# Second feed-forward of an attention kernel: one tile at a time, or two tiles side by side

## The chip, the cores and the metric

The kernel runs on one core of a Trainium2 chip. The metric is the device time of one execution in microseconds (us). The engines are TensorE (PE; its weight loads are PEld), VectorE (DVE), ScalarE (ACT), GpSimd (POOL) and SyncE (SP), whose queue issues all DMA of this kernel.

## The reference

Attention within chunks of 64 tokens, then two feed-forwards on 4608 tokens of width 512. The change is in the second one, which takes `x`, the first one's output:

```
def _moe2_ref(x, w1, w2, w3, w_out):      # x: 4608 x 512
    a = x @ w1                            # 512 x 1024
    b = x @ w2                            # 512 x 1024
    h = a * b @ w3                        # 1024 x 1024
    return (h @ w_out).astype(np.float32) # 1024 x 512
```

Both kernels fold `w3 @ w_out` into one matrix of 1024 x 512 beforehand, so this stage is `(a * b) @ wf`.

## The kernel before

Every fp32 number is split into a high and a low part, and each product of matrices runs as three matmuls into one accumulation: high by high, high by low, low by high (`mm3`, lines 105 to 107). `split` (lines 100 and 101) makes the parts, the high one on ACT, the low one on DVE.

The 4608 tokens are 9 tiles of 512. The second feed-forward goes through the tiles in the order `PASS2` = 8, 2, 3, 4, 5, 6, 7, 0, 1, and in each tile through 8 units `f`, each of them 128 columns of `w1` and of `w2`: 72 units `u`. In a unit, the two products `a` and `b` are computed together by the scheme of Strassen and Winograd on 2 x 2 blocks: seven block products instead of eight. The blocks of the token operand are the two halves of the width by the two halves of the tile, so a block has 256 tokens, and sums of blocks are formed once per tile: `B11`, `B21`, `T2`, `T1`, `T3`, `B22`, `T4`, the seven operands `X`. The four weight operands of a unit are blocks of `w1`, `w2` and sums of them. They are prepared in an earlier stage, stored in DRAM (`sd`), and loaded once by `pump()`, line 316: three tiles `w` of 512 KB and one tile `s4` of 256 KB per unit. For all 8 units that is 24 of the 25 `w` slots, and there they stay for all tiles.

`ab_mm(u)` issues the seven products of a unit: 7 x 2 x 3 = 42 matmuls that move 256 columns. They go into four PSUM banks of two pools (`ps_hh`, `ps_aa`), which ACT (`x1`, line 474) and DVE (`d`, `e`, lines 482 to 501) empty while they combine the products. Line 662 multiplies `a` by `b`. `ab_split(u)` splits the result into one of the two halves of the ring `phl`. `out_mm(u - 1)` then issues the output product of the unit before: 4 accumulators `acc` x 3 = 12 matmuls that move 512 columns of `wf`. At the last unit of a tile each accumulator is copied into an `o` tile (even ones by ACT, odd ones by DVE; three buffers) and stored.

So PE's order in the steady state is 42 narrow matmuls of unit u, 12 wide ones of unit u - 1, and so on. At a tile's last unit `x_op` is called behind each product and overwrites the operand just used with that of the next tile; the sums for it were made by POOL (`x_sums`).

Order on each engine is program order: the stage is under a manual schedule, and each engine's queue is served in the order in which the code issues. In the first unit the last output product of the first feed-forward (`x2_mm`, 24 wide matmuls) lies between.

Of the kernel before, what the change touches and what calls it, by code (L numbers as in the profile page):

```python
# [17 lines left out]
P = 128  # L18
NT = 4608
TT = 512  # L20
# [25 lines left out]
ORDER3E = "S1sT25a3cACoobBoxodoDyoo"  # L46
ORDER3X = "12sq5a3clhAbCrmdBDxy"
FOLD = 1
N3 = 13


# [4 lines left out]
def chunk_attention_two_ffn(  # L56
# [246 lines left out]
    def pump():  # L303

        n = 0
        while lq and lq[0] in staged:
            key = lq[0]
            if key[1] == 3 and isinstance(key[0], tuple):
                if not free(s4s, 1):
                    break  # L310
                t = new_s4(key)
            elif free(slots, 1):
                t = new_w(key)
            else:
                break
            nc.sync.dma_start(out=f32(t), in_=staged.pop(lq.pop(0)))
            n += 1
        return n


    qks, vs, att = {}, {}, {}
# [294 lines left out]
    def fold(b, part):  # L616

        if part == 0:
            wf_ps[b] = bank_a()
        a = W["w3", 2 * b + part // 2]  # L620
        for j in range(2 * part, 2 * part + 2):
            o = W["wo2", j]
            m = slice(P * (j % 4), P * (j % 4) + P)
            mm3(wf_ps[b], (a[:, 0, m], a[:, 1, m]), (o[:, 0], o[:, 1]), j == 0, j == 7)
        if part % 2:
            load_w3()
        if part == 3:
            hi, lo = (one.tile([P, TT], F32R, tag=tag, name="wfo") for tag in ("s5", "s6"))
            p = wf_ps.pop(b)
            nc.scalar.activation(hi, p, AF.Copy)  # L630
            nc.vector.tensor_tensor(out=lo, in0=p, in1=f32(hi), op=ALU.subtract)
            nc.sync.dma_start(out=wfd[b][:, 0], in_=f32(hi))
            nc.sync.dma_start(out=wfd[b][:, 1], in_=f32(lo))
            if b == FB2 - 1:
                done_with(("wo2", j) for j in range(FB2))
                done_with(["x2o"])


    order = PASS2
    phv, phl = {}, {}  # L640

    def load_wf(f):
        if f in (2, 3):
# [7 lines left out]
            parts = d[:, 0], d[:, 1]  # L651
        W["wf", f] = parts

    def ab_mm(u):
        f = u % FB2
        last = f == FB2 - 1 and u + 1 < NTILE * FB2
        z = Seven(("w12", f), (bank_h, bank_h, bank_a, bank_a), True, x_op if last else None)
# [5 lines left out]
        phv[u] = z.e  # L663

    def ab_split(u):
        if u == 0:
            phl["both"] = one.tile([P, 8, 256], F32R, tag="g", name="phl")
        t = phl["both"][:, 4 * (u % 2):4 * (u % 2) + 4].rearrange("p (s t) k -> p s (t k)", s=2)
        split(t, phv.pop(u), nc.vector)
        phl[u] = t  # L670

    def out_mm(u):
        n, f = order[u // FB2], u % FB2
# [3 lines left out]
        w, p = W["wf", f], phl.pop(u)  # L677
        for b in range(4):
            m = slice(P * b, P * b + P)
            mm3(acc[b], (p[:, 0, m], p[:, 1, m]), w, f == 0, f == FB2 - 1)  # L680
            if f == FB2 - 1:
                t = wk.tile([P, TT], F32, tag="cw", name="o", bufs=3)
                if b % 2 == 0:
                    nc.scalar.activation(t, acc[b], AF.Copy)
                else:
                    nc.vector.tensor_copy(t, acc[b])
                r0 = n * TT + b * P
                nc.sync.dma_start(out=out[r0:r0 + P, :], in_=t)


    with tc.manual_schedule():
# [34 lines left out]
        for i in range(NG):  # L726
            if i == GA:
                sq.extend(("wo2", j) for j in range(FB2))
                for g in range(GA, G1):
                    sq.extend((nm, 2 * g + e) for nm in ("in", "out") for e in range(2))  # L730
                    lq.extend((("in", g), p_) for p_ in range(4))
                    lq.extend(("out", 2 * g + e) for e in range(2))
                lq.extend(("wo2", j) for j in range(FB2))
                sq.extend(("w3", j) for j in range(N3))
                for f in range(FB2):
                    sq.extend((nm, f) for nm in ("w1", "w2"))
                    if N3 + f < 16:
                        sq.append(("w3", N3 + f))
                    lq.extend((("w12", f), p_) for p_ in range(4))
                st_load()  # L740
            if i == iB + FOLD - 1:
                load_w3()
# [78 lines left out]
            if ps == 1:  # L821
                if nth == 0 and nxt in xs:
                    if not pre:
                        xr = one.tile([P, CC, TT], F32R, tag="xf", name="xr")
                        pre.update((op, xr[:, 2 * j:2 * j + 2]) for j, op in enumerate(("B11", "B21")))
                    for op in pre:
                        nc.sync.dma_start(out=f32(pre[op]), in_=xs[nxt][op])
                if nth == 0 and nxt not in xs:
                    if pre:
                        pre.clear()  # L830
                        xf = one.tile([P, CC, TT], F32, tag="xf", name="xf")
                    nc.sync.dma_start(out=xf, in_=x2d[order[0]] if nxt is None else xd[nxt])
# [6 lines left out]
        U2 = NTILE * FB2  # L839
        for f in (4, 5, 6):  # L840
            load_wf(f)
        for u in range(U2 + 1):
            if u < FB2:
                need(*((("w12", u), p_) for p_ in range(4)))
            pump()
            if u == FB2 - 1:
                load_wf(FB2 - 1)
            if u < U2:
                ab_mm(u)
                if u == 0:  # L850
                    x2_mm(NG - 1, 0)
                    x2_mm(NG - 1, 1)
                ab_split(u)
            if u >= 1:
                out_mm(u - 1)
            if u == 0:
                load_wf(2)
                load_wf(3)
            f = u % FB2
            if u < U2 - FB2:  # L860
                if f == 1:
                    nc.sync.dma_start(out=xf, in_=x2d[order[u // FB2 + 1]])
                if f == 4:
                    x_sums()


# [47 lines left out]
```

## Time and profile before

| | |
|---|---|
| timed runs | 1526.86, 1527.42, 1532.41 us; median 1527.42 |
| span of the profiled execution, first to last instruction | 1524.5 us |
| time of the profiled execution by the clock of the timed runs | not recorded; the span lies 2.9 us below the median |
| PE busy | 1470.5 us, 96% of the span |
| DVE, ACT, POOL busy | 1099.5, 773.8 and 261.8 us |
| DMA | 248.82 MB, 163 GB/s over the span |

The profile records one execution. A busy matmul in it is counted from its start to its modelled end, and the next one starts before that end, so how fast PE works is read from the distances between starts, and whether it works without a pause from its list of waits.

### The profile page before, as it was taken

What the parts mean: (1) busy time and instruction counts of PE and PEld (TensorE: products, weight loads), DVE (VectorE), ACT (ScalarE), POOL (GpSimd) and SP (SyncE); (2) the same over time, 40 slices, a digit from 0 to 9 for tenths busy, and PEclk for the clock granted to TensorE, in tenths of its full rate; (3) what the DMA queues carried; (4) which work ended last, traced back from release to release, by engine and by line L of the source; (5) the groups of instructions that cost most, each with busy time, mean ns of one, the idle gap of its engine ahead of it and who ended that gap; (6) DMA issues with size and microseconds to landing.
All of it is one profiled execution on the core that took longest, in us unless ns stands there. A gap on an engine that the chain in (4) does not pass through costs nothing.

```text
span 1524.5 us, 28710 instructions
## 1 busy us (share of the span) xinstructions
PE 1470.5 (96%) x11340; PEld 1318.9 (87%) x11340; DVE 1099.5 (72%) x1876; ACT 773.8 (51%) x1349; POOL 261.8 (17%) x206
## 2 busy tenths in 40 slices
PE   4789999999999999999999999999999999999998
PEld 3778788888888889888888888999999999999998
DVE  6986798888888887777777777665655646656564
ACT  4877788787887876555555556221221212212121
POOL 0222222222222222222221122101101011010000
PEclk7999999999999999999999999999999999999999
DMA  7654655565664718998888775601101101011000
GB/s 241 204 198 141 213 174 204 163 243 193 213 212 138 242 63 310 359 328 320 299 315 299 274 279 191 258 9 48 56 1 56 37 20 57 1 56 56 1 29 28
DMA packets 103814, 248.82 MB, mean 163 GB/s; under 512 B 11520, under 2 KB 23552, under 8 KB 102016
## 3 DMA queue, kind: packets, MB, share of 16 engines
q1 hardware_dynamic: 103680, 246.99, 46.9%
q8 instruction: 90, 1.47, 0.4%
q14 instruction: 44, 0.36, 0.1%
HBM read 151.78 MB, written 95.16 MB: 162 GB/s over the span
## 4 chain that ended last, share of the span: by engine, by line
PE 68%; DVE 12%; ACT 12%; DMA 5%; issue 2%; POOL 1%; SPq 0%; DVEq 0%; ACTq 0%; POOLq 0%
PE acc L106 9%; PE acc L105 9%; PE acc L107 9%; PE ps_hh L105 9%; PE ps_hh L107 8%; PE ps_hh L106 8%; PE ps_aa L105 5%; PE ps_aa L106 5%; PE ps_aa L107 5%; ACT t L551 2%; ACT L368 2%; ACT t L550 1%; ACT L551 1%; POOL ex L377 1%; DVE ex L362 1%
## 5 line engine op out<-in xcount | busy, mean ns | idle before, releaser
L564 POOL TENSOR_TENSOR g<-t,g 128x512 fp32r<-128x512 f32 x144 | 196.5, 1385 | 584.4 <-ACT g L563 464.4
L100 ACT ACTIVATE phl<-e 128x512 fp32r<-128x512 f32 x72 | 45.5, 632 | 364.8 <-DVE e L662 356.7
L105 PE MATMUL acc<-g,w 128*128 128x512 f32 x576 | 228.1, 396 | 0.0
L106 PE MATMUL acc<-g,w 128*128 128x512 f32 x576 | 226.8, 394 | 0.1
L107 PE MATMUL acc<-g,w 128*128 128x512 f32 x576 | 224.8, 390 | 0.0
L107 PE MATMUL ps_hh<-T,w 128*128 128x256 f32 x680 | 193.3, 284 | 4.7 <-DVE w L198 4.7
L105 PE MATMUL ps_hh<-T,w 128*128 128x256 f32 x680 | 196.8, 289 | 0.9 <-ACT x L474 0.9
L106 PE MATMUL ps_hh<-T,w 128*128 128x256 f32 x680 | 193.1, 284 | 0.0
L105 PE MATMUL ps_hh<-B,w 128*128 128x256 f32 x620 | 180.2, 291 | 5.1 <-DVE t L555 3.3
L482 DVE TENSOR_TENSOR d<-x,ps_hh 128x512 f32<-128x512 f32 x134 | 91.8, 685 | 120.6 <-PE ps_hh L107 103.7
L106 PE MATMUL ps_hh<-B,w 128*128 128x256 f32 x620 | 176.7, 285 | 0.0
L107 PE MATMUL ps_hh<-B,w 128*128 128x256 f32 x620 | 176.6, 285 | 0.0
L107 PEld LDWEIGHTS ps_hh<-T,w 128*128 128x128 f32 x680 | 131.0, 193 | 5.3 <-DVE w L198 5.1
L105 PEld LDWEIGHTS ps_hh<-T,w 128*128 128x128 f32 x680 | 131.0, 193 | 4.5 <-ACT x L474 1.5
L106 PEld LDWEIGHTS ps_hh<-T,w 128*128 128x128 f32 x680 | 131.1, 193 | 0.7
L105 PEld LDWEIGHTS ps_hh<-B,w 128*128 128x128 f32 x620 | 119.7, 193 | 12.4 <-DVE t L555 3.8
L107 PEld LDWEIGHTS acc<-g,w 128*128 128x128 f32 x576 | 108.3, 188 | 22.9
L106 PEld LDWEIGHTS acc<-g,w 128*128 128x128 f32 x576 | 108.6, 189 | 22.2 <-POOL g L564 3.1
L105 PEld LDWEIGHTS acc<-g,w 128*128 128x128 f32 x576 | 108.6, 188 | 19.5
L106 PEld LDWEIGHTS ps_hh<-B,w 128*128 128x128 f32 x620 | 119.9, 193 | 3.9
L106 PE MATMUL ps_aa<-T,w 128*128 128x256 f32 x432 | 122.5, 284 | 0.4 <-DVE T L101 0.4
L107 PE MATMUL ps_aa<-T,w 128*128 128x256 f32 x432 | 122.4, 283 | 0.0
(139 smaller groups left out, 3598.4 us busy)
## 6 DMA issues: line engine op xcount, KB each, us to landing
w<-sd SPq DMA_DIRECT2D x63, 512.0 KB, 7.3
sd<-raw SPq DMA_DIRECT2D x104, 256.0 KB, 4.4
qk<-in_q_dram SPq DMA_DIRECT2D x36, 256.0 KB, 4.2
qk<-in_k_dram SPq DMA_DIRECT2D x36, 256.0 KB, 4.6
vt<-in_v_dram SPq DMA_DIRECT2D x72, 128.0 KB, 3.0
x2a<-x2o SPq DMA_DIRECT2D x36, 256.0 KB, 2.6
x2a<-x2a SPq DMA_DIRECT2D x36, 256.0 KB, 5.5
x2d<-x2a SPq DMA_DIRECT2D x36, 256.0 KB, 3.1
```

Source lines behind the costliest of these rows:

```text
L100: nc.scalar.activation(dst[:, 0], src, AF.Copy)
L105: nc.tensor.matmul(ps, a[0], b[0], start=first, stop=False)
L106: nc.tensor.matmul(ps, a[0], b[1], start=False, stop=False)
L107: nc.tensor.matmul(ps, a[1], b[0], start=False, stop=last)
L362: nc.vector.tensor_tensor(out=ex[:, :, c], in0=ps[c], op=ALU.subtract, in1=mx[:, :, c].unsqueeze(2).to_broadcast([P, HP, 64]))
L368: nc.scalar.activation(ex, ex, AF.Exp, scale=SCALE)
L377: (nc.vector if early else nc.gpsimd).tensor_tensor(out=ex, in0=ex, in1=rc.unsqueeze(2).to_broadcast([P, 2 * HP, 64]), op=ALU.mult)
L482: nc.vector.tensor_tensor(out=two(self.d), in0=self.x1.unsqueeze(1).to_broadcast([P, 2, 256]), in1=two(p26), op=ALU.add)
L550: nc.scalar.activation(t, t, AF.Abs)
L551: nc.scalar.activation(t, t, AF.Sin, scale=-TWO_PI, bias=half_pi)
L564: nc.gpsimd.tensor_tensor(out=lo, in0=r, in1=f32(hi), op=ALU.subtract)
```

## The change

Tile 8 is still done alone, by `alone_mm`, as before. The other eight tiles are taken in pairs: (2, 3), (4, 5), (6, 7), (0, 1). The blocks of the token operand are now the two halves of the width by the two tiles of the pair, so that a block has 512 tokens, and each of the seven products moves 512 columns and fills one PSUM bank. Each operand has two tiles of 512 columns, one per 128 rows of the half width (`X2`): the old `X[op]`, and one more `w` slot.

For each unit of a pair `duo_mm` issues 42 matmuls of 512 columns. The first tile's result is split into the ring at once and goes to `out_mm`, 12 matmuls, behind the products of the following unit. The second tile's result is kept in `pst` (four `w` slots). After the 8 units, the eight output products of the second tile follow one upon the other, each behind a `late_split` of the kept result, and in the same steps the operands of the next pair are split (`duo_op`).

The slots that hold `X2`, `pst` and the sources of a pair (`duo_load`) leave ten for weights. So the weights of all 8 units are no longer resident: `pump()` loads those of a unit again for every pair, at most `AHEAD` = 2 units ahead of the unit in work, and `release(u)` frees a unit's slots when its products are issued.

```diff
     def pump():
         n = 0
-        while lq and lq[0] in staged:
+        while lq:
             key = lq[0]
+            kept = (("w12", key[0][1] % FB2), key[1]) if key[0][0] == "w12" else key
+            if kept not in staged or (kept != key or key[0][0] == "w12") and key[0][1] > unit[0] + AHEAD:
+                break
...
-            nc.sync.dma_start(out=f32(t), in_=staged.pop(lq.pop(0)))
+            nc.sync.dma_start(out=f32(t), in_=staged[kept])
+            lq.pop(0)
             n += 1
...
+    def duo_load(duo):
+        a, b = duo
...
+        nc.sync.dma_start(out=y["A"], in_=x2d[a])
+        nc.sync.dma_start(out=y["lo"], in_=x2d[b][:, 0:2])
+        nc.sync.dma_start(out=y["hi"], in_=x2d[b][:, 2:4])
+
+    def duo_sums():
+        b11, b21, b12, b22, t1, t2 = y["A"][:, 0:2], y["A"][:, 2:4], y["lo"], y["hi"], spare, y["t2"]
+        nc.gpsimd.tensor_tensor(out=t1, in0=b12, in1=b11, op=ALU.subtract)
+        nc.gpsimd.tensor_tensor(out=t2, in0=b22, in1=t1, op=ALU.subtract)
+        nc.gpsimd.tensor_tensor(out=b12, in0=b22, in1=b12, op=ALU.subtract)
+        y["v"] = dict(B11=b11, T1=t1, T3=b12, B21=b21, T2=t2, B22=b22, T4=b21)
+
+    def duo_op(op, c):
+        v = y["v"]
+        split(X2[op][c], v[op][:, c], nc.vector)
+        if op == "T2":
+            nc.vector.tensor_tensor(out=v["T4"][:, c], in0=v["B21"][:, c], in1=v["T2"][:, c], op=ALU.subtract)
+
+    def duo_mm(u, j):
+        f = u % FB2
+        w = [W[("w12", u), i] for i in range(4)]
+        def prod(a, i, op):
+            ps = (bank_h, bank_a)[n_bank[0] // 2 % 2]()
+            n_bank[0] += 1
+            for c in range(2):
+                m = slice(256 * i + P * c, 256 * i + P * c + P)
+                mm3(ps, (w[a][:, 0, m], w[a][:, 1, m]), (X2[op][c][:, 0], X2[op][c][:, 1]), c == 0, c == 1)
+            return ps
...
+        nc.scalar.activation(x1, prod(0, 0, "B11"), AF.Copy)
+        add(d0, x1, prod(0, 1, "B21"))
+        add(d1, x1, prod(2, 0, "T2"))
+        p7 = prod(2, 1, "T3")
+        add(e0, d1, p7)
+        add(e0, e0, prod(1, 1, "T4"))
+        nc.vector.tensor_tensor(out=e0, in0=d0, in1=e0, op=ALU.mult)
+        t = ring(j)
+        nc.scalar.activation(t[:, 0], e0, AF.Copy)
+        add(e1, d1, prod(1, 0, "T1"))
+        add(d1, e1, p7)
+        nc.vector.tensor_tensor(out=t[:, 1], in0=e0, in1=f32(t[:, 0]), op=ALU.subtract)
+        add(e1, e1, prod(3, 0, "B22"))
+        nc.vector.tensor_tensor(out=pst[f // 2][:, f % 2], in0=d1, in1=e1, op=ALU.mult)
+
+    def late_split(j, f):
+        split(ring(j), pst[f // 2][:, f % 2], nc.vector)
...
-        for u in range(U2 + 1):
-            if u < FB2:
-                need(*((("w12", u), p_) for p_ in range(4)))
...
+        for u in range(FB2):
+            take_weights(u)
...
+            e = alone_mm(u, after)
...
+            if u:
+                out_mm(u - 1, *jobs[u - 1])
...
+            release(u)
+            if u == 1:
+                duo_load(DUOS[0])
...
+            if u == 3:
+                duo_sums()
+            if u in (4, 5, 6):
+                for op in (OPS[0:3], OPS[3:5], OPS[5:7])[u - 4]:
+                    duo_op(op, 1)
+        j = FB2
+        for s, duo in enumerate(DUOS):
+            for f in range(FB2):
+                u = FB2 * (s + 1) + f
+                take_weights(u)
+                duo_mm(u, j)
...
+                out_mm(j - 1, *jobs[j - 1])
+                release(u)
+                if s + 1 < len(DUOS):
+                    if f == 1:
+                        duo_load(DUOS[s + 1])
+                    if f == 4:
+                        duo_sums()
+                j += 1
+            late_split(j, 0)
+            for f in range(FB2):
+                out_mm(j - 1, *jobs[j - 1])
+                if f + 1 < FB2:
+                    late_split(j + 1, f + 1)
+                for op, c in halves[2 * f:2 * f + 2]:
+                    duo_op(op, c)
+                j += 1
+        out_mm(j - 1, *jobs[j - 1])
```

How this moves instructions, engine by engine. First PE, in the kernel before, in a unit of the second feed-forward: the end of the seventh product (`T4`) and the first two accumulators of the output.

```order
L105 MATMUL ps_aa<-T_172,w 128x256
L106 MATMUL ps_aa<-T_172,w 128x256
L107 MATMUL ps_aa<-T_172,w 128x256
L105 MATMUL acc_16175<-wf,phl 128x512
L106 MATMUL acc_16175<-wf,phl 128x512
L107 MATMUL acc_16175<-wf,phl 128x512
L105 MATMUL acc_16176<-wf,phl 128x512
L106 MATMUL acc_16176<-wf,phl 128x512
```

The same place in the changed kernel, in a unit of a pair: the seventh product is now `B22`, with the weight tile `s4` (printed `s`), and its second operand tile stands in a `w` slot.

```order
L106 MATMUL ps_aa_15247<-B22_171,s4_15032 128x512
L107 MATMUL ps_aa_15247<-B22_171,s4_15032 128x512
L108 MATMUL ps_aa_15247<-B22_171,s4_15032 128x512
L106 MATMUL ps_aa_15247<-w_11481,s4_15032 128x512
L107 MATMUL ps_aa_15247<-w_11481,s4_15032 128x512
L108 MATMUL ps_aa_15247<-w_11481,s4_15032 128x512
L106 MATMUL acc0_14752<-wf_11280,phl_11369 128x512
L107 MATMUL acc0_14752<-wf_11280,phl_11369 128x512
L108 MATMUL acc0_14752<-wf_11280,phl_11369 128x512
```

The narrow matmuls are gone from there: one wide matmul stands for the two narrow ones of two tiles, and PE has 8738 rows instead of 10082.

Next DVE, in the kernel before, around the end of a tile: the unit's combination, the split (line 101), and the two output copies (line 686) between units.

```order
L501 TENSOR_TENSOR e<-e,ps_aa 128x512
L662 TENSOR_TENSOR e<-d,e 128x512
L101 TENSOR_TENSOR phl<-e,phl 128x512
L686 COPY o<-acc_15589 128x512
L686 COPY o<-acc_15591 128x512
L482 TENSOR_TENSOR d<-x_16125,ps_hh 128x512
L492 TENSOR_TENSOR e<-d,ps_aa 128x512
```

DVE in the changed kernel, at the end of a pair's units, where the second tile's outputs begin: line 750 keeps the last result, line 102 is the split of a kept result (`phl<-w`) or of half an operand of the next pair, line 688 the two output copies of the first tile, line 718 the `T4` subtraction.

```order
L750 TENSOR_TENSOR w<-d_14346,e_14348 128x512
L102 TENSOR_TENSOR phl<-w,phl 128x512
L688 COPY o<-acc_13885 128x512
L688 COPY o<-acc_13887 128x512
L102 TENSOR_TENSOR phl<-w,phl 128x512
L102 TENSOR_TENSOR B_166<-xa_11469,B_166 128x512
L102 TENSOR_TENSOR w<-xa_11469,w 128x512
L102 TENSOR_TENSOR phl<-w,phl 128x512
L102 TENSOR_TENSOR B_167<-xa_11469,B_167 128x512
L102 TENSOR_TENSOR w<-xa_11469,w 128x512
L102 TENSOR_TENSOR phl<-w,phl 128x512
L102 TENSOR_TENSOR T_168<-w,T_168 128x512
```

The copies now stand between the splits of two neighbouring output steps, and operand halves stand between the splits of the later ones.

Last SP's queue, in the kernel before, at the start of the stage: the last weights that are ever loaded (`w`, `s4`), the next tile's source, the last block of `wf`, and the first tile's four stores.

```order
L646 DMA wf_11412<-wfd3_157 128x512
L646 DMA wf_11413<-wfd3_157 128x512
L316 DMA w_11416<-sd28_10389 128x1024
L316 DMA s4_11418<-sd29_10393 128x512
L862 DMA xf_10344<-x2d2_142 128x2048
L650 DMA w_11842<-wfd7_161 128x1024
L688 DMA out_0_dram<-o_11988 128x512
L688 DMA out_0_dram<-o_11994 128x512
```

SP's queue in the changed kernel, at the end of a pair: the weights of a unit ahead, four stores of the first tile, four of the second, and the next unit's weights.

```order
L320 DMA w_12686<-sd42_8746 128x1024
L320 DMA w_12688<-sd42_8928 128x1024
L320 DMA w_12690<-sd43_8932 128x1024
L320 DMA s4_12692<-sd44_8936 128x512
L690 DMA out_0_dram<-o_12699 128x512
L690 DMA out_0_dram<-o_12705 128x512
L690 DMA out_0_dram<-o_12711 128x512
L690 DMA out_0_dram<-o_12717 128x512
L690 DMA out_0_dram<-o_12921 128x512
```

Where the queue held only tile sources and stores after the first tile, weight loads now stand between them to the last pair.

## Rows read from the trace of the kernel before

**Rows 1.** Page: span, PE, and granted clock by slice.

```profile
span 1524.5 us, 28710 instructions
...
PE 1470.5 (96%) x11340; PEld 1318.9 (87%) x11340; DVE 1099.5 (72%) x1876; ACT 773.8 (51%) x1349; POOL 261.8 (17%) x206
...
PEclk7999999999999999999999999999999999999999
```

**Rows 2.** PE's waits, 930 to 1524 us: who, for whom, total, times, longest.

```profile
PE ps_aa L106 <- DVE T L101: 0.4, 1, 0.4
```

**Rows 3.** Timeline of PE, one unit: start, duration, instruction.

```profile
1307.17 0.28 PE L105 MATMUL ps_hh<-B,w 128*128 128x256 f32 x1
...
1312.20 0.40 PE L105 MATMUL acc<-wf,phl 128*128 128x512 f32 x1
...
1313.59 0.39 PE L105 MATMUL acc<-wf,phl 128*128 128x512 f32 x1
...
1314.95 0.28 PE L105 MATMUL ps_hh<-B,w 128*128 128x256 f32 x1
```

**Rows 4.** Timeline of PE, 24 output matmuls of the first unit, ninth and successor.

```profile
961.23 0.39 PE L107 MATMUL acc<-g,w 128*128 128x512 f32 x1
...
964.85 0.28 PE L105 MATMUL ps_hh<-B,w 128*128 128x256 f32 x1
```

**Rows 5.** Windows: busy time by engine, granted clock, DMA share, GB/s.

```profile
960.00:965.00 5.00, 5.00 (x25) 4.13 (x24) 3.52 (x6) 0.00 (x0) 0.00 (x0) 1.00 1.02 409
965.00:970.00 5.00, 5.00 (x44) 5.00 (x43) 3.23 (x6) 1.01 (x2) 0.00 (x0) 1.00 1.03 370
...
1300.00:1350.00 50.00, 50.00 (x354) 47.06 (x353) 29.96 (x48) 11.55 (x22) 3.09 (x3) 1.00 0.12 43
```

**Rows 6.** Groups by line, second feed-forward; last, POOL's one sum at 983 us.

```profile
L101 DVE TENSOR_TENSOR phl<-e,phl 128x512 fp32r<-128x512 f32 x63 | 44.0, 698 | 44.0 <-ACT phl L100 44.0
...
L100 ACT ACTIVATE phl<-e 128x512 fp32r<-128x512 f32 x63 | 39.8, 632 | 317.0 <-DVE e L662 317.0
...
L438 POOL TENSOR_TENSOR xf<-xf x1: 1298/1298/1298, 983.3 to 983.3; 128x512 f32<-128x512 f32 x1
```

**Rows 7.** Timeline of DVE: two independent operations, then two dependent ones.

```profile
1078.66 0.69 DVE L101 TENSOR_TENSOR T<-spare,T 128x512 fp32r<-128x512 f32 x1
1079.26 0.69 DVE L101 TENSOR_TENSOR T<-xf,T 128x512 fp32r<-128x512 f32 x1
...
1094.57 0.69 DVE L501 TENSOR_TENSOR e<-e,ps_aa 128x512 f32<-128x512 f32 x1 [0.29 <-PE ps_aa L107]
1095.29 0.69 DVE L662 TENSOR_TENSOR e<-d,e 128x512 f32<-128x512 f32 x1
```

**Rows 8.** Timeline of the kernel's end: accumulator copies and stores.

```profile
1517.23 0.39 PE L105 MATMUL acc<-w,phl 128*128 128x512 f32 x1
...
1518.13 0.60 ACT L684 ACTIVATE o<-acc 128x512 f32<-128x512 f32 x1 [1.36 <-PE acc L107]
...
1518.75 3.21 SPq L688 DMA_DIRECT2D out_dram<-o  x4
...
1519.74 0.39 PE L107 MATMUL acc<-w,phl 128*128 128x512 f32 x1
1520.91 0.69 DVE L686 COPY o<-acc 128x512 f32<-128x512 f32 x1 [1.41 <-DMA out_dram<-o]
```

**Rows 9.** Line 688 (output stores), 1000 to 1524 us.

```profile
DMA to landing us min/median/max: 2.0/2.1/4.3
```

**Rows 10.** Line 316 (weight loads), 930 to 980 us.

```profile
DMA to landing us min/median/max: 3.7/7.4/10.1
```

**Rows 11.** Timeline of SP's queue near the first unit's end.

```profile
966.18 1.10 SPq L646 DMA_DIRECT2D wf<-wfd  x2
...
970.66 0.80 SPq L646 DMA_DIRECT2D wf<-wfd  x2
971.51 0.42 SPq L316 DMA_DIRECT2D w<-sd  x1
```

More of the change, by code (lines that the diff above doesn't have):

```diff
@@ L48 @@
 FOLD = 1
+AHEAD = 2
 N3 = 13
@@ L315, in pump @@
                 break
-            nc.sync.dma_start(out=f32(t), in_=staged.pop(lq.pop(0)))
+            nc.sync.dma_start(out=f32(t), in_=staged[kept])
+            lq.pop(0)
             n += 1
         return n
+    unit = [0]
     qks, vs, att = {}, {}, {}
@@ L635, in fold @@
                 done_with(("wo2", j) for j in range(FB2))
-                done_with(["x2o"])
-    order = PASS2
-    phv, phl = {}, {}
+    ALONE, DUOS = PASS2[0], [(2, 3), (4, 5), (6, 7), (0, 1)]
+    UNITS = FB2 * (1 + len(DUOS))
+    phl = {}
     def load_wf(f):
@@ L652, in load_wf, with ring, alone_mm @@
         W["wf", f] = parts
[L654 to L657, printed above, removed]
+    def ring(j):
+        if not phl:
+            phl["both"] = one.tile([P, 8, 256], F32R, tag="g", name="phl")
+        return phl["both"][:, 4 * (j % 2):4 * (j % 2) + 4].rearrange("p (s t) k -> p s (t k)", s=2)
+    def alone_mm(u, after):
+        z = Seven(("w12", u), (bank_h, bank_h, bank_a, bank_a), True, after)
         z.step1()
@@ L662, in ab_mm, with out_mm @@
         nc.vector.tensor_tensor(out=z.e, in0=z.d, in1=z.e, op=ALU.mult)
[L663 to L673, printed above, removed]
+        return z.e
+    def out_mm(j, n, f):
         if f == 0:
@@ L676, in out_mm @@
                 acc[b] = ps_acc.tile([P, TT], F32, tag=f"acc{b}", name=f"acc{b}")
-        w, p = W["wf", f], phl.pop(u)
+        w, p = W["wf", f], ring(j)
         for b in range(4):
@@ L688, in out_mm @@
                 nc.sync.dma_start(out=out[r0:r0 + P, :], in_=t)
+    DUO = ("B11", "B21", "T2", "T3", "T4", "T1", "B22")
+    X2, y, pst = {}, {}, []
+    n_bank = [0]
+    def duo_load(duo):
+        a, b = duo
+        if "lo" not in y:
+            y["A"] = one.tile([P, CC, TT], F32, tag="xf", name="xa2")
+            y["lo"], y["hi"], y["t2"] = (f32(new_w(("duo", i))) for i in range(3))
+        nc.sync.dma_start(out=y["A"], in_=x2d[a])
+        nc.sync.dma_start(out=y["lo"], in_=x2d[b][:, 0:2])
+        nc.sync.dma_start(out=y["hi"], in_=x2d[b][:, 2:4])
@@ new lines, in duo_mm, with add @@
+    def duo_mm(u, j):
[8 more added lines that the diff above has]
+            return ps
+        def add(o, a, b):
+            nc.vector.tensor_tensor(out=o, in0=a, in1=b, op=ALU.add)
+        x1, d0, d1, e0, e1 = (one.tile([P, TT], F32, tag=tag, name=name) for tag, name in
+                              (("s7", "x1"), ("d", "d0"), ("s5", "d1"), ("e", "e0"), ("s6", "e1")))
+        nc.scalar.activation(x1, prod(0, 0, "B11"), AF.Copy)
[12 more added lines that the diff above has]
+        nc.vector.tensor_tensor(out=pst[f // 2][:, f % 2], in0=d1, in1=e1, op=ALU.mult)
@@ L738, in chunk_attention_two_ffn @@
                         sq.append(("w3", N3 + f))
-                    lq.extend((("w12", f), p_) for p_ in range(4))
+                lq.extend((("w12", u), p_) for u in range(UNITS) for p_ in range(4))
                 st_load()
@@ L831, in chunk_attention_two_ffn @@
                         xf = one.tile([P, CC, TT], F32, tag="xf", name="xf")
-                    nc.sync.dma_start(out=xf, in_=x2d[order[0]] if nxt is None else xd[nxt])
+                    nc.sync.dma_start(out=xf, in_=x2d[ALONE] if nxt is None else xd[nxt])
                 if end:
@@ L838, in chunk_attention_two_ffn, with release, take_weights @@
         split_g(NG - 1)
-        U2 = NTILE * FB2
         for f in (4, 5, 6):
             load_wf(f)
-        for u in range(U2 + 1):
-            if u < FB2:
-                need(*((("w12", u), p_) for p_ in range(4)))
+        def release(u):
+            done_with((("w12", u), p_) for p_ in range(4))
+            unit[0] = u + 1
+            pump()
+        def take_weights(u):
+            need(*((("w12", u), p_) for p_ in range(4)))
+        jobs = [(ALONE, f) for f in range(FB2)]
+        jobs += [(n, f) for duo in DUOS for n in duo for f in range(FB2)]
+        for u in range(FB2):
+            take_weights(u)
             pump()
@@ L847, in chunk_attention_two_ffn @@
                 load_wf(FB2 - 1)
[L848 to L855, printed above, removed]
+                after = lambda op: duo_op(op, 0)
+            else:
+                after = None
+            e = alone_mm(u, after)
+            if u == 0:
+                x2_mm(NG - 1, 0)
+                x2_mm(NG - 1, 1)
+            split(ring(u), e, nc.vector)
+            if u:
+                out_mm(u - 1, *jobs[u - 1])
             if u == 0:
@@ L858, in chunk_attention_two_ffn @@
                 load_wf(3)
[L859 to L864, printed above, removed]
+            release(u)
+            if u == 1:
+                duo_load(DUOS[0])
+                X2.update((op, (X[op], new_w(("X2", op)))) for op in OPS)
+                pst.extend(f32(new_w(("pst", i))) for i in range(4))
+            if u == 3:
[9 more added lines that the diff above has]
+                duo_mm(u, j)
+                if f == FB2 - 1 and s + 1 < len(DUOS):
+                    halves = [(op, c) for op in DUO for c in range(2)]
+                else:
+                    halves = []
+                out_mm(j - 1, *jobs[j - 1])
[15 more added lines that the diff above has]
+        out_mm(j - 1, *jobs[j - 1])
 def _layout(inputs):
```

## The prediction

> **What bounds the kernel now.** I read the page first: TensorE (PE) is busy 1470.5 of 1524.5 us and its granted clock is at the top level, 2.4 GHz, in every slice but the first [rows 1]. A busy share can hide gaps, because matmuls overlap, so I asked next for PE's own waits from 930 us on, which takes in the whole second feed-forward: one is left, of 0.4 us [rows 2]. So PE streams without a pause to the end, and the time of this stage is a number of matmuls times their distance. Vector (DVE), Scalar (ACT) and the DMA have room: in 1300 to 1350 us DVE is busy 29.96 of 50 us, ACT 11.55, and the DMA moves 43 GB/s [rows 5].
>
> So the third view is the timeline of one unit, read by start times and not by durations [rows 3]. The 42 product matmuls of 256 columns take from 1307.17 to 1312.20: 5.03 us, 0.1198 each. The 12 output matmuls of 512 columns take to 1314.95: 2.75 us, 0.2292 each. The whole unit is 7.78 us. Inside the 12 there are two paces: the first six, just behind the narrow ones, take 1.39 us (0.2317 each), the last six 1.36 us (0.2267 each). A long run shows which pace lasts: in the 24 output matmuls of the first unit, the 16 from 961.23 to 964.85 take 3.62 us, 0.2263 each [rows 4], while the DMA moves 409 GB/s in that stretch [rows 5]. Streaming 256 columns more thus costs 0.2267 - 0.1198 = 0.1069 us, and each matmul carries 0.013 us besides, whatever its width.
>
> **The change part by part.**
>
> *Products.* Four pairs of tiles with 8 units each run 42 x 32 = 1344 matmuls of 512 columns in place of 2688 of 256. By the lasting pace: 2688 x 0.1198 = 322.0 us go, 1344 x 0.2267 = 304.7 come: -17.3 us. I take 0.2267 since a pair's whole stretch is 512 columns wide; the slower six are only seen behind a narrow run. For the same reason the 768 output matmuls of the pairs go from 0.2292 to 0.2267: -1.9 us. Counted in units, without the rounding, it is 2 x 7.78 - 66 x 0.2267 = 0.598 us, 32 times: -19.1 us. Bounds: with 0.2317 everywhere the products give -10.6 and the outputs +1.9, so -8.7; with 0.2263 it is -20. The tile that stays alone keeps its 8 units at 7.78 us.
>
> A rule weighed here. The Trainium skill, "TensorE: Matmul & The Clock Gate", section "Back-to-back issue gap", gives a warm matmul a gap of its columns over 2.4 plus 2.5 ns. By it a merged pair saves 2.5 ns and the change 1344 x 0.0025 = 3.4 us. The rows show 13 ns at both widths, so by the measured unit the saving is five times that; what else sits in the 13 ns they do not say.
>
> *Weights.* They no longer stay resident: each unit of a pair loads three tiles of 512 KB and one of 256 KB, 1.84 MB, again. 32 units make 59 MB more. A unit's products and its 12 outputs last 54 x 0.2267 = 12.24 us, so 150 GB/s are wanted, and half of every pair wants none; the stretch at 409 GB/s shows that the queue can do it, and that PE keeps its pace meanwhile. Unit u frees the slots for unit u + 3, so a load has about two units, 24 us, to land; such loads landed in 3.7 to 10.1 us when the DMA was full [rows 10]. Cost 0. If the cover were gone, PE would lose in every unit what the load is late.
>
> In the tile that is alone units last 7.78 us, so 236 GB/s and a lead of 15 us: still covered. Only unit 3 is close. Its loads stand in SP's queue behind the last two `wf` loads, which before went out at 970.66 to 971.46, as they wait for buffers whose stores must land [rows 11]. Unit 3 begins at 964.85 + 2 x 7.78 = 980.4, so 9 us behind an issue at 971.5, against a median landing of 7.4 and at most 10.1. But before, the loads of units 3 to 7 were filling the DMA at that time, and now they are not. Between 0 and 1.1 us, once; I take 0.5.
>
> *Operands of the first pair.* Their 2 MB are loaded behind the weights of units 3 and 4, at about 974 us; with 3.7 MB ahead at 370 to 409 GB/s they land at about 984 to 989. Three Pool sums of 1024 columns follow, at twice 1.30 us each (a 512-column one takes 1.298 [rows 6]); T2 is there after two, at 989 to 994. The wait that is added: ACT's copy of T2 stands ahead of unit 5's `x1` in ACT's queue, at about 996, and `x1` frees a PSUM bank for PE. Covered by 2 us at the late end; each us more costs one, once. I take 0.
>
> *Second halves.* Eight output steps in a row without products: 12 x 0.2267 = 2.72 us each. Behind each, DVE and ACT owe one split of the stored product, and in seven of the eight steps two halves of the next pair's operands. DVE starts independent operations 0.60 us apart and dependent ones 0.72 [rows 7]: three operations are 1.8 us, the T2 step with its two T4 subtractions about 3.2. That step overruns by 0.5 us, and the next, again 1.8, takes it up; the split has a step of lead, since the ring has two halves and the chain from PE's end over ACT (0.63) and DVE (0.70) [rows 6] needs 1.5 of 2.72. Cost 0; without that lead 0.5 us per pair.
>
> *The turn from the first tile to the second.* Output of the last block (f = 7) is now followed at once by output of f = 0, into the same four accumulators; before, 5 us of products lay between. The tail of the kernel shows the timing [rows 8]. Counted from the first of the 12 matmuls (1517.23; the last starts at 1519.74): first copy at +0.90, its store issued at +1.52; the copy of the fourth accumulator waits for that store, as there are three `o` buffers, and runs from +3.68 to +4.37. The next step writes that accumulator at 2.72 + 2.04 = +4.76. So 0.4 us of slack with a store that lands in 2.1 us; at the longest, 4.3 [rows 9], PE would lose 1.8 us, at four turns 7.3. The pair's last weights are issued some 5 us earlier and should have landed, so I take 0.5 for all four.
>
> *Removed for nothing.* Operand splits at 8 tile boundaries, hidden (no wait in [rows 2]); the same elements are split now. Pool, ACT and DVE totals stay about equal.
>
> Sum: 1524.5 - 19.1 + 0.5 + 0.5 = 1506.4 us of span. The three timed runs have a median of 1527.42, 2.9 above the profiled span, so I forecast **1509 us**. A measurement of this kernel tells about 0.5% (7.6 us) from no change.
>
> **The rivals.**
> 1. *Store-bound turns*: the `o` stores land late among the weights. For it: the median store landed in 2.1, one in 4.3 us [rows 9]. Against: little else moves then. 1506.4 - 0.5 + 7.3 of span, so about 1516.
> 2. *Loads late in the alone tile*: unit 3's weights or the first pair's sums are late by 1 to 6 us in all. For it: nine us of lead against 10.1. Against: the DMA has less to do before that. 1510 to 1515.
> 3. *The wide matmul keeps the slow pace* of 0.2317: -8.7, so 1520. Against: [rows 4].
> 4. *The change saves next to nothing*: the 13 ns belong to every 256 columns of the X operands, so that a merged product costs 2 x 0.1198 and only the outputs gain their 1.9: 1525. For it: no 512-column read of X stands in the trace. Against: 512 columns of other operands carry it once. The rule above ends close by, at 1524.
> 5. *Slower: DVE becomes the bound of the second halves.* Splits and operand halves share one queue; if one step takes longer than PE's 2.72 us, each step adds the difference. It would have to add more than 19.1 + 7.6 = 26.7 us in the 21 loaded steps of three pairs: 1.3 us a step, so 4.0 us for what I count as 1.8. For it: DVE waits for ACT inside each split, and once they stop overlapping, 3 x (0.63 + 0.70) = 4.0 us is just that. Against: their inputs wait in SBUF, so ACT runs ahead. About 1535.
>
> **How the numbers follow.** Forecast 0.70, rival 1 0.10, rival 2 0.08, rival 3 0.03, rival 4 0.05, rival 5 0.04. The range 1506 to 1517 holds the first three: its low end is the sum at the fastest pace and without the two halves of a us (1507.4), less the 0.6 by which the fastest timed run lies under the median, rounded down; its high end is rival 1. Faster by over 0.5%: the first three, 0.88; within: rivals 3 and 4, 0.08; slower: 0.04.
>
> **What would show it.** In the changed profile a pair's product matmul starts 0.227 us behind the one before, one unit with its outputs lasts 12.24 us, eight output steps 21.8. A PE wait for DVE or ACT on `acc` at the turn speaks for rival 1; one for a DMA into `w` or for ACT's `x1` between 980 and 1005 us for rival 2; a wait for `phl` in each output step for rival 5; a start distance of 0.232 without waits for rival 3. I am wrong if wide matmuls on the X operands start further apart than wide ones on `wf`, or if the pairs' stretch shows waits of more than a few us.

## The result, and the profile after

The changed kernel takes 1509.3 us (median of four runs, 1507.3 to 1515.81), the kernel before took 1529.91 beside it (1526.86 to 1532.5): a ratio of 0.9878, with a 95% interval of 0.986 to 0.9897. By that ratio it is 19 us less, between 16 and 21. The forecast was 1509, with 18.1 us less.

The profiled execution is the slowest of the four, 1515.81 us, with a span of 1514.0. Its first lines on the page, which answer to [rows 1]:

```profile
span 1514.0 us, 26149 instructions
...
PE 1455.7 (96%) x9996; PEld 1251.1 (83%) x9996; DVE 1099.8 (73%) x1844; ACT 766.9 (51%) x1317; POOL 262.0 (17%) x194
...
PEclk9999999999999999999999999999999999999999
```

PE has 1344 matmuls fewer (9996 against 11340); DVE and POOL are busy as long as before, ACT 7 us less. The span alone would say that only 10.5 us were gained. So I compared the stage by itself, from the first product of its second unit, which is the matmul behind the 24 output matmuls of the first feed-forward. In the timeline of PE (start, duration, instruction) it is the last row here, at 971.52, where [rows 4] has it at 964.85:

```profile
971.29 0.39 PE L108 MATMUL acc<-g,w 128*128 128x512 f32 x1
971.52 0.28 PE L106 MATMUL ps_hh<-B,w 128*128 128x256 f32 x1
```

From there to the end it is 1524.5 - 964.85 = 559.7 us before and 1514.0 - 971.52 = 542.5 after: 17.2 less. The other 6.7 us were lost ahead of the stage, in parts that issue the same work in both kernels; in the eight experiments below, which share those parts with the changed kernel, the last of the 24 matmuls starts between 963.46 and 966.05 us, in this execution at 971.29. Why they took longer here is not known. All times of the stage below are counted from that point, so that this does not enter.

One unit of a pair, in the timeline of PE, against [rows 3]: the start of its last product, its first output, the next unit's first product and that unit's last product.

```profile
1202.78 0.39 PE L106 MATMUL ps_aa<-B,s 128*128 128x512 f32 x1
...
1204.14 0.39 PE L106 MATMUL acc<-wf,phl 128*128 128x512 f32 x1
...
1206.86 0.39 PE L106 MATMUL ps_aa<-B,w 128*128 128x512 f32 x1
...
1215.02 0.39 PE L106 MATMUL ps_hh<-B,s 128*128 128x512 f32 x1
```

From `B22` to `B22` it is 12.24 us, 54 matmuls at 0.2267; the 12 outputs take 2.72; the six of a product (1202.78 to 1204.14) 1.36. The first of a run is no slower than the last: the slow start behind narrow matmuls is gone with them.

PE's waits from 940 us on, against [rows 2]:

```profile
PE acc L106 <- DVE o L688: 1.5, 1, 1.5
PE ps_aa L107 <- DVE T L102: 0.4, 1, 0.4
```

The 0.4 us were there before. The 1.5 us are new. They stand at the last of the four turns from a pair's first tile to its second; the timeline of DVE, ACT and SP there, which answers to [rows 8]:

```profile
1483.82 0.60 ACT L686 ACTIVATE o<-acc 128x512 f32<-128x512 f32 x1 [0.21 <-PE acc L108]
...
1484.44 5.18 SPq L690 DMA_DIRECT2D out_dram<-o  x4
...
1488.57 0.69 DVE L688 COPY o<-acc 128x512 f32<-128x512 f32 x1 [3.38 <-DMA out_dram<-o]
```

The fourth accumulator's copy waits 3.38 us for the first store to land, which took 3.9 us in place of 2.0. At the three other turns the same copy came 2.22 to 2.23 us behind the store's issue, and PE did not wait. In PE's row the copy's end is followed by the matmul that had to wait:

```profile
1487.47 0.39 PE L108 MATMUL acc<-wf,phl 128*128 128x512 f32 x1
1489.32 0.50 PE L106 MATMUL acc<-wf,phl 128*128 128x512 f32 x1 [1.46 <-DVE o L688]
1489.66 0.40 PE L107 MATMUL acc<-wf,phl 128*128 128x512 f32 x1
```

1489.32 - 1487.47 = 1.85 us instead of 0.23, and the next distance is 0.34: 1.7 us lost.

The weights that are loaded again, in the landing times of line 320 from 1030 us on, against [rows 10], and in the windows view (busy us of PE, PEld, DVE, ACT, POOL with counts, granted clock, DMA share, GB/s), against [rows 5]:

```profile
DMA to landing us min/median/max: 3.2/4.1/11.0
```

```profile
1200.00:1250.00 50.00, 50.00 (x222) 41.39 (x222) 29.31 (x45) 8.73 (x15) 0.00 (x0) 1.00 0.44 148
1250.00:1300.00 50.00, 50.00 (x222) 41.41 (x221) 32.01 (x48) 13.79 (x25) 3.38 (x2) 1.00 0.43 161
```

The DMA moves 148 to 161 GB/s where it moved 43, PE is never idle in these stretches, and its list of waits has no load.

### The profile page after: what moved, and what is told of

It reads as the page before. It is cut to its first block, busy times and chain, and to the rows that moved or that the text cites. A ratio compares the mean times of both kernels' runs of the same rounds, so it can differ in the third digit from the quotient of the medians.

```text
span 1514.0 us, 26149 instructions
## 1 busy us (share of the span) xinstructions
PE 1455.7 (96%) x9996; PEld 1251.1 (83%) x9996; DVE 1099.8 (73%) x1844; ACT 766.9 (51%) x1317; POOL 262.0 (17%) x194
## 4 chain that ended last, share of the span: by engine, by line
PE 65%; ACT 12%; DVE 12%; DMA 7%; issue 2%; POOL 1%; SPq 0%; DVEq 0%; ACTq 0%; POOLq 0%
PE ps_hh L106 9%; PE acc L107 8%; PE acc L106 8%; PE acc L108 8%; PE ps_hh L108 8%; PE ps_hh L107 8%; PE ps_aa L107 4%; PE ps_aa L106 4%; PE ps_aa L108 4%; ACT t L558 2%; DMA sd<-raw 2%; ACT L375 2%; ACT t L557 2%; ACT L558 1%; POOL ex L384 1%
## 5 line engine op out<-in xcount | busy, mean ns | idle before, releaser
L108 PE MATMUL ps_hh<-T,w 128*128 128x256 f32 (+1 forms) x616 | 182.2, 296 | 6.3 <-DVE w L199 6.2
L106 PE MATMUL ps_hh<-T,w 128*128 128x256 f32 (+1 forms) x616 | 185.3, 301 | 0.5 <-ACT x L481 0.5
L107 PE MATMUL ps_hh<-T,w 128*128 128x256 f32 (+1 forms) x616 | 181.8, 295 | 0.0
L108 PEld LDWEIGHTS ps_hh<-T,w 128*128 128x128 f32 x616 | 118.6, 193 | 9.4 <-DVE w L199 6.9
L106 PE MATMUL ps_hh<-B,w 128*128 128x256 f32 (+1 forms) x396 | 120.4, 304 | 5.3 <-DVE t L562 3.3
L106 PEld LDWEIGHTS ps_hh<-T,w 128*128 128x128 f32 x616 | 118.6, 192 | 6.4 <-ACT x L481 0.9
L745 ACT ACTIVATE phl<-e 128x512 fp32r<-128x512 f32 x32 | 20.2, 633 | 201.5 <-DVE e L743 201.5
L107 PEld LDWEIGHTS ps_hh<-T,w 128*128 128x128 f32 x616 | 118.6, 193 | 3.2
L107 PE MATMUL ps_hh<-B,w 128*128 128x256 f32 (+1 forms) x396 | 116.6, 294 | 0.0
L108 PE MATMUL ps_hh<-B,w 128*128 128x256 f32 (+1 forms) x396 | 116.4, 294 | 0.0
L558 ACT ACTIVATE t<-t,half_pi 128x512 f32<-128x512 f32 x144 | 104.3, 724 | 4.0
L106 PE MATMUL acc<-wf,phl 128*128 128x512 f32 x252 | 98.2, 390 | 1.5 <-DVE o L688 1.5
L107 PE MATMUL acc<-wf,phl 128*128 128x512 f32 x252 | 98.1, 389 | 0.0
L108 PE MATMUL acc<-wf,phl 128*128 128x512 f32 x252 | 98.0, 389 | 0.0
L547 ACT ACTIVATE t<-d 128x512 int32<-128x512 f32 x62 | 38.9, 628 | 115.8 <-DVE d L501 115.8
```

The lines of the kernel that those rows point to most:

```text
L106: nc.tensor.matmul(ps, a[0], b[0], start=first, stop=False)
L107: nc.tensor.matmul(ps, a[0], b[1], start=False, stop=False)
L108: nc.tensor.matmul(ps, a[1], b[0], start=False, stop=last)
L547: nc.scalar.activation(t.bitcast(I32), h, AF.Copy, scale=INV2PI)
L558: nc.scalar.activation(t, t, AF.Sin, scale=-TWO_PI, bias=half_pi)
L745: nc.scalar.activation(t[:, 0], e0, AF.Copy)
```

## The experiments

Each kernel is the changed one with one edit. "Stage" is the time from the second unit's first product to the end, 559.7 us before and 542.5 in the changed kernel. A "late turn" is a turn at which PE waits for a late store, as above. Where no median is named, the kernel ran once, and its total can be off by the several us by which executions differ; the stage, read from that execution's trace, says more.

### Wide products issued as halves

```diff
-            for c in range(2):
-                m = slice(256 * i + P * c, 256 * i + P * c + P)
-                mm3(ps, (w[a][:, 0, m], w[a][:, 1, m]), (X2[op][c][:, 0], X2[op][c][:, 1]), c == 0, c == 1)
+            for h in range(0, TT, 256):
+                t = slice(h, h + 256)
+                for c in range(2):
+                    m = slice(256 * i + P * c, 256 * i + P * c + P)
+                    mm3(ps[:, t], (w[a][:, 0, m], w[a][:, 1, m]), (X2[op][c][:, 0, t], X2[op][c][:, 1, t]), c == 0, c == 1)
```

> Everything as in the changed kernel, pairs, reloads and order of the outputs too, but each product of a pair is issued as two matmuls of 256 columns in place of one of 512. Theory (each matmul carries a fixed 13 ns besides its columns): 1344 x (2 x 0.1198 - 0.2267) = 17 us come back, and the outputs behind narrow runs start slower again, so about 18 us more than the changed kernel, ratio to the kernel before 0.998 to 1.001. Rival (the gain comes from the order: fewer operand turns, outputs in a row, fewer PSUM evacuations): the time stays near 1509, ratio 0.988.

Measured: median 1528.27 us of ten runs, ratio to the kernel before 1.0009 (0.9993 to 1.0024). The stage takes 1527.1 - 965.96 = 561.1 us, 18.6 more than the changed kernel, and both executions have one late turn. The timeline of PE shows the old distance inside a pair, 0.12 us:

```profile
1200.69 0.28 PE L106 MATMUL ps_aa<-T,w 128*128 128x256 f32 x1
1200.81 0.28 PE L107 MATMUL ps_aa<-T,w 128*128 128x256 f32 x1
1200.93 0.28 PE L108 MATMUL ps_aa<-T,w 128*128 128x256 f32 x1
```

So pairs, reloads, fewer evacuations and the new order of outputs are together worth nothing that shows: the stage is 1.4 us longer than before, about its late turn. The gain is in the width of the matmul, and with it in half the number of matmuls and of weight loads; this run does not part these. The rival on the order falls.

### Wide products issued as quarters

The same edit with 128 in place of 256.

> As the run with halves, but four matmuls of 128 columns for each of 512. Theory of a fixed cost for each matmul: 128 columns start 0.0667 us apart, so 1344 x (4 x 0.0667 - 0.2267) = 54 us more than the changed kernel, about 1563. Rival (at 256 columns the pace is set by the weight load, which has the same size for any width): 128 columns start 0.12 us apart as well, 1344 x (4 x 0.12 - 0.2267) = 340 us more, about 1850.

Measured: 1805.59 us; stage 838.4, 296 us more than the changed kernel. The timeline of PE and of its weight loads:

```profile
1301.18 0.27 PE L107 MATMUL ps_hh<-w 128*128 128x128 f32 x1
1301.29 0.28 PE L108 MATMUL ps_hh<-w 128*128 128x128 f32 x1
1301.40 0.28 PE L106 MATMUL ps_hh<-B,w 128*128 128x128 f32 x1
```

```profile
1301.12 0.19 PEld L107 LDWEIGHTS ps_hh<-w 128*128 128x128 f32 x1
1301.23 0.19 PEld L108 LDWEIGHTS ps_hh<-w 128*128 128x128 f32 x1
1301.34 0.19 PEld L106 LDWEIGHTS ps_hh<-B,w 128*128 128x128 f32 x1
```

128 columns start 0.111 us apart, barely sooner than 256 (0.120), and the weight loads keep the same beat. My theory of a fixed cost on top of the columns fails here: it gives 0.067. In its place stands a floor of about 0.111 us for each matmul, all of which have a weight load of their own. With the mean of all narrow ones, 0.1113, the products take 1344 x (4 x 0.1113 - 0.2267) = 294 us more; the outputs, slower at first behind narrow matmuls, take 4 more, and the changed kernel's late turn (1.7) is missing: 296, as measured. The Trainium skill, "TensorE: Matmul & The Clock Gate", section "LDWEIGHTS (loading the stationary operand)", gives a load 107 ns for 128 weight columns, however many rows they have; the trace agrees with a beat of 111. The Trainium skill's section "Back-to-back issue gap", on the same page, gives 128 columns 56 ns for an isolated matmul and about 81 ns in a stream with weight loads; here the measurement says 111.

### Wide products issued as 384 and 128 columns

> Each wide product as one matmul of 384 columns and one of 128, first the six wide ones of a product, then the six narrow ones. Theory A (a matmul starts 13 ns plus its columns after the last, but never sooner than about 112 ns, the floor that the run with quarters showed): 384 columns start 0.173 us apart, 128 columns 0.112, so 1344 x (0.285 - 0.2267) = 78 us more than the changed kernel, about 1587. Theory B (the 13 ns at 256 columns are that floor seen from below, and wider matmuls carry something else): 384 columns start at another distance, 0.160 without a fixed cost or 0.167 with half of it, and the time is 9 to 18 us lower than by theory A.

Measured: 1595.56 us; stage 1593.8 - 963.79 = 630.0, 87.5 more than the changed kernel. Of these, 82 lie in the products, for which theory A has 78 and theory B 60 to 69; 2 come from a late turn that was dearer than the changed kernel's (last section), and the rest from the outputs behind narrow matmuls. The timeline of PE has a period of six wide and six narrow ones, from first to first 1402.21 - 1400.48 = 1.73 us:

```profile
1400.48 0.39 PE L106 MATMUL ps_aa<-T,w 128*128 128x384 f32 x1
...
1401.60 0.22 PE L106 MATMUL ps_aa<-T,w 128*128 128x128 f32 x1
1401.66 0.27 PE L107 MATMUL ps_aa<-T,w 128*128 128x128 f32 x1
1401.77 0.27 PE L108 MATMUL ps_aa<-T,w 128*128 128x128 f32 x1
...
1402.21 0.39 PE L106 MATMUL ps_aa<-T,w 128*128 128x384 f32 x1
```

Theory A gives 6 x (0.173 + 0.112) = 1.71 for it, theory B 1.63 to 1.67: A is close, and what is left over is on its far side. It is no clean measure of 384 columns, though: behind narrow matmuls the wide ones do not settle within six. The first of six is followed after 0.23 us, the others after 0.17 to 0.19.

### No weights loaded again

The lists of loads end with the tile that is alone, and every unit of a pair uses the weights of that tile's unit 5, 6 or 7, whose slots are kept.

```diff
-                lq.extend((("w12", u), p_) for u in range(UNITS) for p_ in range(4))
+                lq.extend((("w12", u), p_) for u in range(FB2) for p_ in range(4))
...
+            if u >= FB2:
+                W.update(((("w12", u), i), W[("w12", 5 + u % 3), i]) for i in range(4))
```

> The changed kernel without the 59 MB of weights loaded again: all pairs use the weights of the last three units of the tile that is alone, so the products of the pairs have wrong weights. Theory (the loads are covered): the time stays within 2 us of the changed kernel, ratio 0.986 to 0.990, and the matmul distances stay 0.227. Rival (the loads slow matmuls or stores a little everywhere, or make the late stores): faster than the changed kernel by 3 us or more.

Measured: median 1506.12 us, ratio 0.9871 (0.9854 to 0.9889), beside 0.9878 (0.986 to 0.9897) for the changed kernel: not told apart. The stage takes 1504.4 - 963.68 = 540.7 us, 1.8 less than in the changed kernel, whose late turn cost 1.7; this execution had none. The distances are 0.227 in both. Apart from that turn, 59 MB more cost PE nothing that shows. Whether they make late stores more frequent is not shown: this execution had no late store, but neither had the one with quarters, which loads them, and the kernel before, which does not, had several.

### Weights loaded one unit ahead, and none ahead

```diff
-AHEAD = 2
+AHEAD = 1      # the other kernel: 0
```

> The changed kernel with weights loaded at most one unit ahead. Theory (what covers the loads is the reading order of the ten slots, since a load takes the slot that has been free longest; the bound by units matters only where SP's queue is held up by other entries): one wait of about 5 us at the unit that follows the first two, whose loads stand behind the wf loads, and no wait in the pairs; about 1514. Rival (the lead is what the bound says, one unit, 7.8 us in the tile that is alone and 12.2 in the pairs): waits of up to 2 us in each unit of the alone tile, none in the pairs.

Measured with one unit: 1511.64 us; stage 545.0. PE's waits for loads, from 900 us on:

```profile
PE ps_hh L106 <- DMA w<-sd: 2.2, 1, 2.2
```

One place, where unit 2 begins, and nothing in the pairs. By the start distances 4.2 us are lost there: 2.4 in this wait, 0.5 a little later for another tile of the same unit, and the rest because PE then ran at half its clock. The windows (as above) show where it fell:

```profile
975.00:975.70 0.70, 0.64 (x5) 0.67 (x6) 0.00 (x0) 0.00 (x0) 0.00 (x0) 1.00 0.95 380
975.70:979.00 3.30, 3.18 (x15) 2.88 (x14) 0.00 (x0) 0.39 (x1) 0.00 (x0) 0.50 1.04 422
```

The place is as expected and the price near the 5 us; but a third of it is the clock, which the expectation did not have. The wait itself was short, since the `wf` loads ahead went out at 966.25 to 968.11 and no longer at 971. The rival, a wait in each unit of that tile, falls.

> The changed kernel with weights loaded only when the unit before has been issued. Theory (as for the run with one unit): about 12 us at the second unit, and 5 to 7 us at the second unit of each pair, whose loads now stand in SP's queue behind the stores of the tile before, four times; about 1540 to 1550. Rival (every unit waits for its own loads): 32 waits of 4 us or more in the pairs, over 1640.

Measured with none: 1550.59 us; stage 1548.8 - 963.97 = 584.8, counted from where the second unit would have begun, 0.23 us behind the last of the 24 matmuls.

```profile
PE ps_aa L106 <- DMA w<-sd: 23.7, 4, 6.1
PE ps_hh L106 <- DMA w<-sd: 9.1, 1, 9.1
```

One wait at the second unit and one at the second unit of each pair, and none at the others. So the number of units ahead is not what covers the loads in the steady run: a load takes the slot that has been free longest, and can go out long before its unit. The bound matters where SP's queue is held up by earlier entries, and those are the stores of a finished tile. In its timeline the loads leave behind the four stores:

```profile
1040.94 3.21 SPq L690 DMA_DIRECT2D out_dram<-o  x4
1044.21 1.39 SPq L320 DMA_DIRECT2D w<-sd  x3
```

The rival of a wait in every unit falls. Against the run that loads no weights again (540.7, without a wait) the stage is 44.1 us longer; by start distances the five waits are 33.7 of it. The other 10 are the clock again, which was at half behind each of the five (last section).

### A fourth output tile

```diff
-                t = wk.tile([P, TT], F32, tag="cw", name="o", bufs=3)
+                t = (one.tile([P, TT], F32, tag="v", name="o") if b == 3 else
+                     wk.tile([P, TT], F32, tag="cw", name="o", bufs=3))
```

> The changed kernel with a fourth output tile, so that the copy of the fourth accumulator no longer waits for the first store. Theory (a late store at a turn costs up to 1.8 us, and one of four turns had one): no wait of PE for DVE's output copy is left in the profile, and the time falls by 0 to 2 us, to a ratio of 0.987 to 0.989. Rival (that wait only hides another, such as the splits behind the copies): a wait of the same size at the turn, now for the split.

Measured: median 1507.86 us, ratio 0.9881 (0.9866 to 0.9896). No wait for DVE's output copy is left, though three stores at the last turn (1479 to 1481 us) again took 4.0 to 4.1 us to land. The stage takes 1506.3 - 966.28 = 540.0 us: 2.5 less than the changed kernel, 1.7 of it the turn, and 0.7 at the very end, where the last copy no longer waits either (from the last matmul's start to the end 4.35 us, against 5.06). The runs do not tell this kernel from the changed one; the trace does. The rival, a wait of the splits behind, did not come.

### Operand halves bunched

```diff
-                for op, c in halves[2 * f:2 * f + 2]:
+                for op, c in halves[4 * f:4 * f + 4]:
```

> The changed kernel with the operand halves of the next pair put into the first four output steps of the second tile, four in a step, instead of two in each of seven. Theory (DVE starts one operation each 0.60 us and one that follows from the last each 0.72; the T2 step now takes 4.4 us against PE's 2.72, and the ring gives one step of lead): PE waits 1 to 2 us in each of three pairs, for the split of the kept result; about 1512 to 1515. Rival (DVE and ACT have more room than counted): no wait, about 1509.

Measured: 1512.79 us; stage 1511.0 - 964.60 = 546.4, 3.9 more. PE's waits from 900 us on:

```profile
PE acc L108 <- DVE phl L102: 2.4, 3, 0.8
PE acc L106 <- DVE o L688: 1.2, 1, 1.2
```

Three waits for the split, one in each pair whose second half prepares another. With their neighbours they cost 1.3 us a pair, 4.0 in all; a late turn was there as well (1.4). The expected 1 to 2 us hold. In the changed kernel two halves to a step leave DVE idle before the next split (timeline of DVE, first pair):

```profile
1131.24 0.69 DVE L102 TENSOR_TENSOR w<-xa,w 128x512 fp32r<-128x512 f32 x1
1132.69 0.69 DVE L102 TENSOR_TENSOR phl<-w,phl 128x512 fp32r<-128x512 f32 x1 [0.77 <-ACT phl L101]
1133.30 0.69 DVE L102 TENSOR_TENSOR T<-w,T 128x512 fp32r<-128x512 f32 x1
1133.90 0.69 DVE L718 TENSOR_TENSOR xa<-xa,w 128x512 f32<-128x512 f32 x1
```

DVE keeps its 0.60 us also for the subtraction behind the T2 split, which I had counted with 0.72: it reads the split's source and not its result.

## Why the prediction was right

*The number.* That the median met the forecast to 0.3 us is luck: the four runs lie up to 8.5 us apart. The stage is the better measure. There the three terms of the sum, -19.1 + 0.5 + 0.5 = -18.1, stand against 17.2 us less. The 2.9 us that were added from span to time are 1.7 to 1.8 in every run here that has both; the rest was a difference between two executions.

*The pace.* The term was -19.1 us. The stage became 17.2 us shorter although it lost 1.7 in the late turn and 0.3 in a longer end (5.06 against 4.76 us from the last matmul's start); without these two it is 19.2. The choice of the lasting 0.2267 over the first six's 0.2317 was right, and the run with halves shows the cause: with the width taken away, all of the time came back.

*What the 13 ns are.* The prediction read them as a cost of each matmul whatever its width. At 256 and 512 columns that holds and was enough; below, it does not, since a floor of 0.111 us takes over. Nor does it hold at half the clock, where the 13 ns are not there (last section). So 256 columns (0.120) lie just above the floor, and the step from 128 to 256 costs next to nothing, while the step from 256 to 512 saves 13 ns in each pair of matmuls. What the 13 ns consist of stays open: no run here takes the weight load away.

*Rivals 3 and 4* fall with the start distances of 0.2267 on the X operands, and rival 2 with PE's list of waits, which has neither a load nor ACT's `x1`.

*Weights.* Cost 0 was right (no reload: not told apart). The reason was half right: the lead comes from the order in which slots are reused, and the bound matters where SP's queue is held up. A bound of one unit is enough in all pairs; two are needed at unit 2 of the tile that is alone. The half us for unit 3 did not come: its loads went out at 974.74 and the unit began at 971.52 + 2 x 7.78 = 987.1, 12.3 us later, not 9.

*First pair's operands.* Pool's second sum ended at 998.14 us and ACT read it at 1003.67, 5.5 us later. The cover was larger than the 2 us of the late end.

*Second halves.* No wait, as forecast; rival 5 needs more than four halves a step. Four cost 1.3 us a pair, so the lead of one step that the prediction counted on is there, and is used up at about twice the load.

*The turn.* The sum had 0.5 us for four turns; the profile shows 1.7 at one and none at three, so this term was sized too low, and rival 1 is true in kind at a quarter of its price. With a store landing in 3.9 us the slack of 0.4 predicts 1.5. But rival 1 gave the wrong neighbour: no weights were moving then (the DMA moved nothing from 1478 to 1483 us). Of the eight executions with three `o` buffers four had one late turn, and the dearest, with 384 and 128 columns, cost 3.9 us, more than the 1.8 that the prediction took for the most, because the clock fell behind it.

## What to carry to other kernels

Read the pace of a saturated TensorE from start distances at every width the trace has, and look at a long run: with a weight load for each matmul, 128 columns cost 0.111 us here, 256 cost 0.120, and 512 cost 0.227, so a kernel at 256 columns can win 5% of its matmul time by pairing, and one at 128 half of it. When weights are loaded again instead of being kept, look for the entries that hold up the DMA queue, here the stores at the end of a tile, and put the loads of at least the next two units ahead of them (a bound of one unit did that here, and no unit of a pair waited). A buffer ring that hides the median store does not hide the late one: ask what one more buffer costs.

## What the runs showed of the hardware that was not expected

Behind a pause PE can run at half its clock. In the run with no units ahead it came back so from one of its waits of 6 us; timeline and windows of PE there:

```profile
1041.93 0.39 PE L108 MATMUL acc<-w,phl 128*128 128x512 f32 x1
1048.39 0.77 PE L106 MATMUL ps_aa<-B,w 128*128 128x512 f32 x1 [6.07 <-DMA w<-sd]
...
1051.09 0.63 PE L106 MATMUL ps_hh<-B,w 128*128 128x512 f32 x1
1051.51 0.63 PE L107 MATMUL ps_hh<-B,w 128*128 128x512 f32 x1
```

```profile
1030.00:1041.90 11.90, 11.90 (x54) 9.87 (x53) 9.34 (x15) 2.57 (x5) 0.00 (x0) 1.00 0.02 5
1048.00:1053.00 5.00, 4.61 (x11) 3.68 (x12) 0.00 (x0) 0.60 (x1) 0.00 (x0) 0.50 1.03 417
1053.00:1060.00 7.00, 7.00 (x31) 5.76 (x31) 4.27 (x7) 0.63 (x1) 0.00 (x0) 0.99 1.01 394
```

The granted clock is 0.50, 1.2 instead of 2.4 GHz, and 512 columns start 0.427 us apart until 1053. That costs 0.2 us a matmul, 2.3 us here, on top of the 6.2 of the wait.

Shorter pauses did it too, but later, when PE had begun again. With one unit ahead 2.6 us lay between two starts; PE began at the full clock, fell to 0.50 at 975.7 and stayed there to 979.0 (windows above). With 384 and 128 columns 2.36 us lay between two starts at the late turn; windows from its end on:

```profile
1144.40:1145.10 0.70, 0.70 (x3) 0.61 (x4) 0.70 (x2) 0.00 (x0) 0.00 (x0) 1.00 0.00 0
1145.10:1148.00 2.90, 2.90 (x9) 2.28 (x8) 2.85 (x5) 1.67 (x3) 0.00 (x0) 0.51 0.24 90
```

That turn cost 3.9 us by the start distances, 1.6 of it by the clock. The late turns with 1.85 us between starts (changed kernel, halves) and 1.56 us (bunched) left the clock at 1.00.

At half the clock a matmul starts its columns at 1.2 GHz after the last and no 13 ns later: 512 columns 0.427 us, and 256 columns, behind the first wait of the run with no units ahead, (977.86 - 973.59) / 20 = 0.2135.

```profile
973.59 0.42 PE L107 MATMUL ps_hh<-B,w 128*128 128x256 f32 x1
...
977.86 0.40 PE L106 MATMUL ps_aa<-T,w 128*128 128x256 f32 x1
```

Stores of 256 KB, which land in 2.0 us, now and then take 3.4 to 4.4, mostly several in succession: in the kernel before, in the changed kernel and in six of the experiments, at different places, with and without other traffic. Why is open.

The first five wide matmuls behind a run of 256 columns are followed after 0.229 to 0.236 us each, and the later ones after 0.226 on average, at the same positions in every unit of the kernel before. Behind a run of 128 columns the first is followed after 0.30. Why is open too.
